# Fetching the filters of a frequency-domain mixer in groups of 16 and 8 rows, with the copies of their halves spread over four engines

## The chip, the cores and the metric

The kernel runs on one core of a Trainium2 chip. The metric is the device time of one execution in microseconds (us), as a median over runs. Five engines work side by side on the core: TensorE (PE: matmuls; PEld is its loading of weights), VectorE (DVE), ScalarE (ACT), GpSimd (POOL) and SyncE (SP), which here only issues transfers. POOL issues transfers too. Each engine takes its instructions strictly in the order in which they were written, and the Tile framework puts semaphore waits between engines.

## The reference

```python
def _attn_ref(x, filt_r, filt_i):              # x: 8 x 3008 x 256; filters: 1505 x 256
    X = np.fft.rfft(x, axis=1)
    Y = X * (filt_r + 1j * filt_i)[None, :, :]
    return np.fft.irfft(Y, n=x.shape[1], axis=1)

def _moe_ref(x, w_gate, w_val, w_out, rms_g):  # 24064 tokens x 256, hidden size 1536
    xn = x / np.sqrt(np.mean(x * x, axis=-1, keepdims=True) + 1e-06) * rms_g
    g = xn @ w_gate
    return (g / (1.0 + np.exp(-g)) * (xn @ w_val)) @ w_out
```

A circular filter along the sequence, done in the frequency domain, is followed by a gated feed-forward network on every token. Inputs and output are float32; the kernel's matmuls take float16.

## The kernel before, in words

The transform of length 3008 = 64 * 47 is split: a matmul with a table of 64 frequencies (`wa`), a transposition, and for each of the 32 values of `k2` a matmul over the 47 others (`wbp`). The result, complex numbers with real parts on partitions 0 to 63 and imaginary parts on 64 to 127, is multiplied by the filter; two products per piece go back through the inverse tables (`wi`), are transposed again, scaled by RMS and sent through the network.

There are 8 sequences. Sequences 1 to 7 are mixed in the gaps of the network's matmuls on the sequence before, by an order written out by hand (`at(slot, ...)`). Sequence 0 has no network to hide behind: everything it needs comes first, and the first matmul of the network (`pg`, L420) follows. All of the change lies in this opening. Its stages:

1. `x_load` (L189, on POOL) fetches sequence 0 with a cast to float16, in eight transfers. SP fetches the tables `tb` and `wbp`.
2. `f_load` (L464 to L473) fetches the filters. For each of four chunks `c` of eight `k2`, and for the real part `fr[c]` and the imaginary part `fi[c]`, one transfer brings 24 rows of 8 KB to every second partition and two transfers bring 12 reversed rows each, in pieces of 1 KB; chunk 0 has one more of 24 rows of 1 KB. `fr` goes through SP, `fi` through POOL, the last `fi` chunk only after the first copies. The other half of each tile is cleared beforehand (L607, L608, L614, L604).
3. `f_dup` (L475 to L480) copies the 64 partitions of `fr[c]` to its upper half and those of `fi[c]` to its lower half: POOL for chunks 0 and 1 and `fi[3]`, ACT for chunk 2 and `fr[3]`.
4. `wi_group` builds the inverse tables; `at_unit` (L486) does the first transform, evicted by ACT (L492) and DVE (L490); `t1_unit` (L509) transposes in eight groups, evicted by DVE (L511) and ACT (L513).
5. `b_unit(0, i)`, i = 0 to 15: two matmuls (L241) into one of four PSUM banks in turn, then the two products with `fr` (L263) and `fi` (L264) of chunk i // 4. They run on DVE, except units 4, 8 and 11, which ACT first copies to SBUF (`v`, L261) and POOL then multiplies.
6. `bit_unit(i)`: sixteen matmuls (L523, L524), two units sharing a pair of PSUM banks; from i = 5 on, every odd i emits the two units five and four steps back; the last four come at the end. ACT evicts them (L532).
7. `t2_unit` (L543), `n_first` (L364), `q_unit` and the scaling lead to the first `pg`. `w_load` (L582, L583, on POOL) fetches the network's weights, the first two thirds after `b_unit(0, 11)`.

`warm_up(n, ...)` issues n matmuls on zeros, 512 columns each, whose results nobody reads.

Of the kernel before, what the change touches and what calls it, by code (L numbers as in the profile page):

```python
# [33 lines left out]
XC = 6  # L34
NXC = H // XC
KC = 8
FC = (8, 8, 8, 8)


def _make_tables():  # L40
    n2 = np.arange(N2)
    wa = np.zeros((P, P))
    wai = np.zeros((P, P))
    for h in range(2):
        for k2 in range(K2):
            c = np.cos(2 * np.pi * ((n2 * k2) % N2) / N2)
            s = np.sin(2 * np.pi * ((n2 * k2) % N2) / N2)
            r = slice(h * 64, h * 64 + 64)
            wa[r, h * 64 + k2] = c
            wai[h * 64 + k2, r] = c * (1.0 if k2 == 0 else 2.0)  # L50
            if k2 == 0:
                alt = 1.0 - 2.0 * (n2 % 2)
                wa[r, h * 64 + 32] = alt
                wai[h * 64 + 32, r] = alt
            else:
                wa[r, h * 64 + 32 + k2] = -s
                wai[h * 64 + 32 + k2, r] = -2.0 * s
    n1 = np.arange(N1)
    wb = np.zeros((KR, K2, P))
    wi = np.zeros((P, 1, 2, P))  # L60
    re, im = slice(0, N1), slice(SL, SL + N1)
    for k2 in range(K2):
        for s in range(48):

            if s < 24:
                k = k2 + 64 * s
                sign, q = 1.0, 16 + 2 * s
            else:
                if k2 and s == 36:
                    continue  # L70
                j = s - 23 if (s < 36 or not k2) else s - 24
                k = 64 * j - (k2 if k2 else 32)
                sign, q = -1.0, 1 + 2 * (s - 24)
            th = 2 * np.pi * ((n1 * k) % N) / N
            c, sn = np.cos(th), np.sin(th)
            if k == 0 or k == NF - 1:
                sn = np.zeros(N1)
            if k2:
                wb[re, k2, q] = c
                wb[im, k2, q] = sign * sn  # L80
                wb[re, k2, HALF + q] = -sn
                wb[im, k2, HALF + q] = sign * c
            else:
                src = re if s < 24 else im
                wb[src, k2, q] = c
                wb[src, k2, HALF + q] = -sn
                m = 1.0 if k in (0, NF - 1) else 2.0
                z = np.zeros(N1)
                g = (m * c, -m * sn)
                gr, gi = (g, (z, z)) if s < 24 else ((z, z), g)  # L90


                for qq, cols in ((re, 0), (im, 1)):
                    wi[q, 0, 0, qq] = (gr, gi)[cols][0]
                    wi[HALF + q, 0, 0, qq] = (gr, gi)[cols][1]
                    wi[q, 0, 1, qq] = (gr, gi)[cols][1]
                    wi[HALF + q, 0, 1, qq] = (gr, gi)[cols][0]
    f = np.float16
    wf = np.zeros((P, K2, P))
    wf[:, 1:, 0:KR] = wb[:, 1:].transpose(2, 1, 0)  # L100
    wf[:, 0] = wi[:, 0, 0]
    wf = (wf * S_INV_B).astype(f)
    ws = np.concatenate([wf[HALF:P], -wf[0:HALF]], 0)
    wai = (wai * S_INV_A).astype(f)
    r = np.arange(KR)
    to_row = (r % 2) * SL + (r // 2 % 2) * H + r // 4
    pm = np.zeros((KR, P))
    pm[r, to_row] = 1.0
    k = np.arange(P)
    ph = (k % 2) * 64 + (k // 2 % 2) * 32 + k // 4  # L110
    tb = np.zeros((P, 7, P), f)
    tb[:, 0] = wa
    tb[:, 1] = np.eye(P)
    tb[0:KR, 2] = pm * S_INV_B
    tb[:, 3] = wf[:, 0]
    tb[:, 4] = ws[:, 0]
    tb[:, 5] = wai[ph]
    tb[:, 6] = wa[:, ph]
    return {"tb": tb, "wb": wb.astype(f), "wbp": wb[to_row].astype(f)}
# [3 lines left out]
def kernel(  # L123
# [39 lines left out]
    pm = tb[0:KR, 2, :]  # L163
    sgn = glob.tile([P, 1], FP32)
    wi = glob.tile([P, 2, K2, P], FP16)
    fr = [glob.tile([P, n, D], FP32, name="fr%d" % c) for c, n in enumerate(FC)]
    fi = [glob.tile([P, n, D], FP32, name="fi%d" % c) for c, n in enumerate(FC)]
    wg = glob.tile([P, 2, DFF], FP16)
    wv = glob.tile([P, 2, DFF], FP16)
    wo = glob.tile([P, JT, D], FP16)  # L170
# [21 lines left out]
    def bank(i, name):  # L192

        pool, tag = ((psM, "mx"), (psG, "pg"), (psV, "pv"), (psB, "mb"), (psO, "po1"), (psO, "po0"))[i]
        return pool.tile([P, 512], FP32, tag=tag, name=name)
# [30 lines left out]
    def wi_at(q, k):  # L226
        return wi[:, q, k, :] if k else tb[:, 3 + q, :]

    def b_unit(b, i):
        if b:  # L230
            ps = bank(3, "psb")
        else:
            ps = bank((0, 3, 4, 5)[i % 4], "psb")
        ps = ps.rearrange("p (a d) -> p a d", a=2)
        for u in range(2):
            k = 2 * i + u
            if b:
                w, t = late_p["wb"], st[b]["t2"][k // KC][:, k % KC, :]
            else:
                w, t = wbp, st[0]["t2"][k // 4][:, k % 4, :]  # L240
            nc.tensor.matmul(ps[:, u, :], w[:, k, :], t, start=True, stop=True)  # L241
        f1, f2 = filt(2 * i, 2)
        if b:
            s1 = late_p["sp"].tile([P, 2, D], FP16, tag="s1", name="s1")
# [9 lines left out]
            ss = xnp.tile([P, 2, 512], FP16, tag="xn", name="ss")  # L254
            s1, s2 = (ss[:, e, :].rearrange("p (a d) -> p a d", a=2) for e in range(2))
        eng = nc.vector
        if (i in (5, 8, 11, 14)) if b else (i in (4, 8, 11)):
            eng = nc.gpsimd
            v = yp.tile([P, 2, 512], FP32, tag="y", name="v")
            v = v[:, 0, :].rearrange("p (a d) -> p a d", a=2)  # L260
            nc.scalar.activation(out=v, in_=ps, func=AXT.Copy)  # L261
            ps = v
# [106 lines left out]
        return y, pss  # L369

    def y_first(y, pss, dh):
        nc.vector.tensor_scalar(out=y[:, dh, :], in0=pss[dh], scalar1=gsb[:, dh:dh + 1],
                                scalar2=None, op0=ALU.mult)

# [81 lines left out]
            nc.sync.dma_start(prev[:, H - 1, :], o3[64:P, 3, :])  # L456


    NC = K2 // KC

    def raw(src, row, ap):
        return bass.AP(tensor=src.tensor, offset=src.offset + row * D, ap=ap)

    def f_load(c, src, t, p0, eng):  # L464
        lo = 1 if c == 0 else 0
        eng.dma_start(t[p0 + 16:p0 + 63:2, :, :].rearrange("p a d -> p (a d)"),
                      raw(src, c * KC, [[64 * D, 24], [1, KC * D]]))
        for g in range(2):
            eng.dma_start(t[p0 + 1 + 24 * g:p0 + 24 + 24 * g:2, lo:KC, :],
                          raw(src, 64 * (1 + 11 * g) - c * KC - lo,  # L470
                              [[64 * D, 12], [-D, KC - lo], [1, D]]))
        if c == 0:
            eng.dma_start(t[p0 + 1:p0 + 48:2, 0, :], raw(src, 32, [[64 * D, 24], [1, D]]))  # L473

    def f_dup(c):  # L475
        for t, a, e in ((fr[c], HALF, 0), (fi[c], 0, HALF)):
            if c == 2 or (c == 3 and a):
                nc.scalar.activation(out=t[a:a + HALF], in_=t[e:e + HALF], func=AXT.Copy)
            else:
                nc.gpsimd.tensor_copy(out=t[a:a + HALF], in_=t[e:e + HALF])  # L480

    def at_unit(m, dh):
        ps = bank(1 + dh, "pat")
# [10 lines left out]
    def t1_unit(g):  # L494
# [4 lines left out]
        else:  # L499
            dst = t3p.tile([KR, 4, D], FP16, tag="t3", name="t2")  # L500
        st[0]["t2"][g] = dst
        pool, tag = ((psO, "po0"), (psO, "po1"), (psM, "mx"), (psB, "mb"))[g % 4]
        ps = pool.tile([P, 4, D], FP16, tag=tag, name="pt1")
        af = aT.rearrange("p a k -> p (a k)")
        for a in range(4):
            for dh in range(2):
                b0 = dh * H * P
                src = af[:, b0:b0 + 32 * P].rearrange("p (i k) -> p k i", k=K2)[:, 4 * g + a, :]
                nc.tensor.transpose(ps[:, a, ts(dh, P)], src, ident)  # L509
        if g % 2 == 0 or g == 7:  # L510
            nc.vector.tensor_copy(out=dst, in_=ps[0:KR])  # L511
        else:
            nc.scalar.activation(out=dst, in_=ps[0:KR], func=AXT.Copy)  # L513
# [72 lines left out]
    with tc.manual_schedule():  # L586
# [26 lines left out]
        for c in range(1, 4):  # L613
            nc.vector.memset(fr[c][0:HALF], 0.0)  # L614
            zero(fi[c][HALF:P])
        for c in range(4):
            f_load(c, filt_r, fr[c], 0, nc.sync)
            if c < 3:
                f_load(c, filt_i, fi[c], HALF, nc.gpsimd)
        with nc.allow_non_contiguous_dma(reason="one gain a partition"):  # L620
            nc.sync.dma_start(gsb, moe_rms_g.rearrange("(a p) -> p a", p=P))

        warm_up(14, 1)
        for g in range(4):
            wi_group(g)
        for m in range(6):
            for dh in range(2):
                at_unit(m, dh)
            for g in ((4, 5), (6,), (7,), (), (), ())[m]:
                wi_group(g)  # L630
        for i in range(8):
            t1_unit(i)
        f_dup(0)
        f_load(3, filt_i, fi[3], HALF, nc.gpsimd)
        f_dup(1)
        for i in range(16):
            if i == 7:
                f_dup(3)
            b_unit(0, i)
            if i % 2 and i >= 5:  # L640
                bit_unit(i - 5)
                bit_unit(i - 4)
            if i == 4:
                f_dup(2)
            if i == 11:
                w_load(0)
                w_load(1)
        for i in range(12, 16):
# [2 lines left out]
        t2_unit(1, 0)  # L651
        warm_up(2, 0)
        first = n_first()
        q_unit(0, 0)
        y_first(*first, 0)
        scale_split(0, 0)
        y_first(*first, 1)
        t2_unit(2, 1)
        t2_unit(3, 0)
        scale_apply(0, 0, 3)  # L660
        t2_unit(4, 0)
# [143 lines left out]
```

## Time and profile before

| What | Value |
|---|---|
| Median of 4 runs | 907.51 us (905.69 to 909.74) |
| The profiled execution, own time | 903.38 us |
| Its span in the trace | 901.6 us, granted clock 0.99 |
| PE busy in the span | 880.2 us (98%) |
| DVE, ACT, POOL busy | 677.1, 619.4, 391.3 us |
| First transposition of `t1_unit` starts | 16.91 us |
| First product of `b_unit(0, 0)` starts on DVE | 22.33 us |
| Last product of `b_unit(0, 15)` ends on DVE | 41.55 us |
| First `pg` matmul of the network starts | 49.71 us |

The profiled execution took 903.38 us, 4.13 us less than the median of the runs; 1.8 us of it lie outside the span. The shares of busy time are averages over the whole span: PE at 98% is the network's work, while the opening of 49.71 us is a different regime that has to be read from the trace itself.

### The profile page before, as it was taken

The numbers are of one execution on the slowest core, as the hardware profiler recorded it, in microseconds if no ns is written. First come the engines' busy times: TensorE is split into PE (matmuls) and PEld (weight loads), VectorE is DVE, ScalarE is ACT, GpSimd is POOL, SyncE is SP. The second block draws the span as 40 slices with busy tenths as digits, with TensorE's granted clock in tenths as the row PEclk, the third lists the DMA queues.
The fourth block names the chain that finished last, engine by engine and source line by source line (L and its number), as shares of the span: only waits on it lengthen the run. The fifth ranks groups of instructions, "written<-read, shape, count | busy, mean of one in ns | idle before, by whom it ended". The sixth has DMA issues, their size and how long they took to land.

```text
span 901.6 us, 17520 instructions
## 1 busy us (share of the span) xinstructions
PE 880.2 (98%) x6329; PEld 561.6 (62%) x6329; DVE 677.1 (75%) x1075; ACT 619.4 (69%) x1047; POOL 391.3 (43%) x353
## 2 busy tenths in 40 slices
PE   8799999999999999999999999999999999999997
PEld 5566666666666666766666666666666666666554
DVE  8766767788988787888688886888878887555554
ACT  8667666677677766887667766787657765676443
POOL 7842730655635552466325552265514551043300
PEclk9699999999999999999999999999999999999999
DMA  9495725674564436444554347332352232331201
GB/s 205 77 185 166 155 57 176 158 172 91 153 178 103 100 79 196 107 95 121 137 139 112 85 98 197 85 96 82 79 168 74 62 89 53 100 68 47 60 24 47
DMA packets 79746, 100.91 MB, mean 112 GB/s; under 512 B 8096, under 2 KB 56416, under 8 KB 79276
## 3 DMA queue, kind: packets, MB, share of 16 engines
q1 hardware_dynamic: 69276, 83.45, 33.6%
q0 software_dynamic: 10384, 16.35, 11.2%
q8 instruction: 49, 0.80, 0.4%
q14 instruction: 37, 0.30, 0.1%
HBM read 67.67 MB, written 46.78 MB: 127 GB/s over the span
## 4 chain that ended last, share of the span: by engine, by line
PE 85%; issue 5%; DMA 4%; ACT 2%; DVE 2%; POOL 2%; SPq 0%; POOLq 0%; ACTq 0%
PE po L437 25%; PE pg L420 25%; PE pv L420 24%; PE psi L286 3%; PE psb L241 3%; PE psn L318 2%; DMA fr<-in_filt_r_dram 2%; PE psa L204 2%; PE psq L339 1%; DVE o L443 1%; DMA g_tmp<-t 1%; DMA rb<-r_tmp 1%; POOL xc L189 0%; ACT sg L424 0%; DVE hh L425 0%
## 5 line engine op out<-in xcount | busy, mean ns | idle before, releaser
L425 DVE TENSOR_TENSOR hh<-pv,sg 128x512 f16<-128x512 f32 (+1 forms) x576 | 391.4, 680 | 202.7 <-ACT sg L424 90.0
L424 ACT ACTIVATE sg<-pg 128x512 f16<-128x512 f32 (+1 forms) x576 | 338.9, 588 | 230.9 <-PE pg L420 222.9
L437 PE MATMUL po<-wo,hh 128*128 128x256 f16 x2256 | 342.2, 272 | 2.3 <-DVE o L443 1.6
L420 PE MATMUL pg<-xn,wg 128*128 128x512 f16 (+1 forms) x1152 | 337.9, 375 | 0.0
L420 PE MATMUL pv<-xn,wv 128*128 128x512 f16 (+1 forms) x1152 | 337.6, 375 | 0.0
L437 PEld LDWEIGHTS <-hh 128*128 128x128 f16 x2256 | 216.5, 98 | 99.2 <-issue 3.6
L277 POOL TENSOR_TENSOR s<-s,s 128x512 f16<-128x512 f16 x96 | 110.5, 1151 | 285.2 <-DVE s L271 202.5
L420 PEld LDWEIGHTS <-wv 128*128 128x128 f16 x1152 | 112.6, 98 | 131.3 <-issue 0.6
L403 POOL TENSOR_TENSOR xn<-y,rb 128x1024 f16<-128x1024 f32 (+1 forms) x45 | 126.0, 2801 | 45.5 <-DMA rb<-r_tmp 33.7
L420 PEld LDWEIGHTS <-wg 128*128 128x128 f16 x1152 | 109.1, 98 | 12.3 <-issue 0.3
L345 POOL TENSOR_TENSOR rho<-u,mhalf 128x4 f32<-128x4 f32 (+1 forms) x48 | 48.9, 1018 | 83.3 <-DVE u L343 83.3
L291 ACT ACTIVATE t<-psi 96x512 f16<-96x512 f32 x112 | 66.4, 593 | 11.5 <-PE psi L286 5.8
L324 ACT ACTIVATE y<-psn,gsb 128x512 f32<-128x512 f32 (+1 forms) x94 | 63.8, 679 | 9.4 <-PE psn L318 2.3
L271 DVE TENSOR_TENSOR s<-psb,fi 64x512 f16<-64x512 f32 x96 | 65.6, 684 | 3.0
L273 DVE SCALAR_TENSOR_TENSOR s<-psb,fi 64x512 f16<-64x512 f32 x96 | 66.5, 693 | 1.3
L247 DVE TENSOR_TENSOR s<-psb,fr 128x512 f16<-128x512 f32 x96 | 65.4, 681 | 0.0
L330 ACT ACTIVATE sq<-psn 128x512 f16<-128x512 f32 (+1 forms) x94 | 54.7, 582 | 0.0
L209 ACT ACTIVATE t<-psa 128x512 f16<-128x512 f32 x70 | 41.8, 597 | 5.6 <-PE psa L204 2.4
L286 PE MATMUL psi<-s,wi 128*128 128x256 f16 x248 | 45.4, 273 | 0.0
L241 PE MATMUL psb<-t,wb 96*128 96x256 f16 x224 | 43.0, 272 | 1.0 <-DVE s L264 0.9
L286 PEld LDWEIGHTS <-wi 128*128 128x128 f16 x248 | 24.2, 98 | 26.5 <-issue 1.4
L318 PEld LDWEIGHTS <-t 128*128 128x128 f16 x368 | 28.3, 98 | 19.8
(97 smaller groups left out, 518.2 us busy)
## 6 DMA issues: line engine op xcount, KB each, us to landing
out_dram<-o SPq DMA_DIRECT2D x84, 256.0 KB
xc<-in_x_dram POOLq DMA_DIRECT2D x56, 192.0 KB, 6.1
z_tmp<-t SPq DMA_DIRECT2D x28, 384.0 KB
t<-z_tmp SPq DMA_DIRECT2D x28, 384.0 KB
g_tmp<-t SPq DMA_DIRECT2D x56, 192.0 KB
rb<-r_tmp SPq DMA_DIRECT2D x41, 256.0 KB
t<-g_tmp SPq DMA_DIRECT2D x21, 384.0 KB
out_dram<-o SPq DMA_DIRECT2D x12, 192.0 KB
```

Source lines behind the costliest of these rows:

```text
L241: nc.tensor.matmul(ps[:, u, :], w[:, k, :], t, start=True, stop=True)
L247: nc.vector.tensor_tensor(out=s1, in0=ps, in1=f1, op=ALU.mult)
L271: nc.vector.tensor_tensor(out=s2[a], in0=ps[e], in1=f2[e], op=ALU.mult)
L273: nc.vector.scalar_tensor_tensor(out=s2[a], in0=ps[e], scalar=-1.0, in1=f2[e], op0=ALU.mult, op1=ALU.mult)
L277: nc.gpsimd.tensor_tensor(out=s, in0=s1, in1=s2, op=ALU.add)
L286: nc.tensor.matmul(ps[:, u, :], wi_at(q, 2 * i + u), ss[q][:, u, :], start=(q == 0), stop=(q == n - 1))
L291: nc.scalar.activation(out=st[b]["t3"][c][:, 2 * r:2 * r + 2, :], in_=ps[0:KR], func=AXT.Copy)
L403: nc.gpsimd.tensor_tensor(out=xv, in0=yv, in1=rv.unsqueeze(1).to_broadcast([P, 2, n, P]), op=ALU.mult)
L420: nc.tensor.matmul(ps[:, 0:w], wt[:, dt_, ts(jt, P)], xn[:, dt_, 0:w], start=(dt_ == 0), stop=(dt_ == 1))
L424: nc.scalar.activation(out=sg[:, 0:w], in_=pg[:, 0:w], func=AXT.Silu)
L425: nc.vector.tensor_tensor(out=hh[:, 0:w], in0=pv[:, 0:w], in1=sg[:, 0:w], op=ALU.mult)
L437: nc.tensor.matmul(po[s4 // 2][:, s4 % 2, :], hh[:, ts(s4, P)], wo[:, jt, :], start=(jt == 0 and s4 % 2 == 0), stop=(jt == JT - 1 and (s4 ...
```

## The change

`f_load` now fetches both parts of a chunk together, in a group of 16 rows through SP (one transfer of 16 rows of 8 KB and one of 16 reversed rows for each part) and a group of 8 rows through POOL (the same two for each part). One reversed row is still fetched twice; it is now the sixteenth in place of the twelfth, so the table row that carries nothing moves from s = 36 to s = 40. All four chunks are issued ahead of the computation, and the gains `gsb` ahead of them. The copies are called one by one, on ACT, POOL or, for `fr[3]`, as a transfer on SP. Six matmuls of `warm_up` stand before `at_unit(4, 0)`. The first four `b_unit`s' matmuls (`b_mm`) stand between the transposition groups 1 and 2, and groups 4 to 7 come after the products of units 0 and 1. Units 3, 7, 10 and 13 go to POOL in place of 4, 8 and 11. The weights' first two thirds are fetched after unit 13. In the tail `y_first` for the second half and `t2_unit(2)` go from DVE to ACT.

```diff
-        if (i in (5, 8, 11, 14)) if b else (i in (4, 8, 11)):
+        if (i in (5, 8, 11, 14)) if b else (i in (3, 7, 10, 13)):
...
     def y_first(y, pss, dh):
+        if dh:
+            nc.scalar.activation(out=y[:, dh, :], in_=pss[dh], func=AXT.Identity, scale=gsb[:, dh:dh + 1])
+            return
...
-    def f_load(c, src, t, p0, eng):
...
+    def f_load(c):
         lo = 1 if c == 0 else 0
+        for g, n, eng in ((0, 16, nc.sync), (16, 8, nc.gpsimd)):
+            for src, t, p0 in ((filt_r, fr[c], 0), (filt_i, fi[c], HALF)):
+                q = p0 + 16 + 2 * g
+                eng.dma_start(t[q:q + 2 * n - 1:2, :, :].rearrange("p a d -> p (a d)"),
+                              raw(src, c * KC + 64 * g, [[64 * D, n], [1, KC * D]]))
+                q = p0 + 1 + 2 * g
+                eng.dma_start(t[q:q + 2 * n - 1:2, lo:KC, :],
+                              raw(src, 64 * max(g, 1) - c * KC - lo, [[64 * D, n], [-D, KC - lo], [1, D]]))
+                if c == 0 and g:
+                    eng.dma_start(t[p0 + 1:p0 + 48:2, 0, :], raw(src, 32, [[64 * D, 24], [1, D]]))
...
+    def f_dup(c, e, eng):
+        t = (fr, fi)[e][c]
+        a, o = (0, HALF) if e else (HALF, 0)
+        if eng is nc.scalar:
+            eng.activation(out=t[a:a + HALF], in_=t[o:o + HALF], func=AXT.Copy)
+        elif eng is nc.sync:
+            eng.dma_start(t[a:a + HALF], t[o:o + HALF])
+        else:
+            eng.tensor_copy(out=t[a:a + HALF], in_=t[o:o + HALF])
...   (t1_unit)
-        pool, tag = ((psO, "po0"), (psO, "po1"), (psM, "mx"), (psB, "mb"))[g % 4]
+        pool, tag = ((psG, "pg"), (psV, "pv"))[g % 2]
...
-        if g % 2 == 0 or g == 7:
+        if g not in (1, 4):
             nc.vector.tensor_copy(out=dst, in_=ps[0:KR])
...
+        for c in range(4):
+            f_load(c)
...
         for m in range(6):
+            if m == 4:
+                warm_up(6, 0)
...
+        A, G, S = nc.scalar, nc.gpsimd, nc.sync
+        t1_unit(0)
+        t1_unit(1)
+        ps0 = [b_mm(0, i) for i in range(4)]
+        t1_unit(2)
+        t1_unit(3)
+        f_dup(0, 0, A)
+        f_dup(0, 1, G)
+        f_dup(1, 1, G)
+        f_dup(3, 0, S)
         for i in range(16):
+            if i == 5:
+                f_dup(2, 0, A)
+                f_dup(2, 1, G)
+            b_unit(0, i, ps0[i] if i < 4 else None)
+            if i == 0:
+                t1_unit(4)
+                t1_unit(5)
+            elif i == 1:
+                t1_unit(6)
+                t1_unit(7)
+            elif i == 3:
+                f_dup(1, 0, A)
+            elif i == 10:
+                f_dup(3, 1, A)
             if i % 2 and i >= 5:
                 bit_unit(i - 5)
                 bit_unit(i - 4)
-            if i == 11:
+            if i == 13:
                 w_load(0)
                 w_load(1)
...
         first = n_first()
+        y_first(*first, 1)
         q_unit(0, 0)
         y_first(*first, 0)
         scale_split(0, 0)
-        y_first(*first, 1)
-        t2_unit(2, 1)
+        t2_unit(2, 0)
```

More of the change, by code (lines that the diff above doesn't have):

```diff
@@ L36 @@
 KC = 8
-FC = (8, 8, 8, 8)
 def _make_tables():
@@ L68, in _make_tables @@
             else:
-                if k2 and s == 36:
+                if k2 and s == 40:
                     continue
-                j = s - 23 if (s < 36 or not k2) else s - 24
+                j = s - 23 if (s < 40 or not k2) else s - 24
                 k = 64 * j - (k2 if k2 else 32)
@@ L165 @@
     wi = glob.tile([P, 2, K2, P], FP16)
-    fr = [glob.tile([P, n, D], FP32, name="fr%d" % c) for c, n in enumerate(FC)]
-    fi = [glob.tile([P, n, D], FP32, name="fi%d" % c) for c, n in enumerate(FC)]
+    fr = [glob.tile([P, KC, D], FP32, name="fr%d" % c) for c in range(K2 // KC)]
+    fi = [glob.tile([P, KC, D], FP32, name="fi%d" % c) for c in range(K2 // KC)]
     wg = glob.tile([P, 2, DFF], FP16)
@@ L227, in wi_at, with b_mm @@
         return wi[:, q, k, :] if k else tb[:, 3 + q, :]
[L229 to L234, printed above, removed]
+    def b_mm(b, i):
+        ps = bank(3 if b else (0, 3, 4, 5)[i % 4], "psb").rearrange("p (a d) -> p a d", a=2)
         for u in range(2):
@@ L241, in b_unit @@
             nc.tensor.matmul(ps[:, u, :], w[:, k, :], t, start=True, stop=True)
+        return ps
+    def b_unit(b, i, ps=None):
+        if ps is None:
+            ps = b_mm(b, i)
         f1, f2 = filt(2 * i, 2)
@@ L456, in o_store @@
             nc.sync.dma_start(prev[:, H - 1, :], o3[64:P, 3, :])
-    NC = K2 // KC
     def raw(src, row, ap):
         return bass.AP(tensor=src.tensor, offset=src.offset + row * D, ap=ap)
-    def f_load(c, src, t, p0, eng):
+    def f_load(c):
         lo = 1 if c == 0 else 0
[L466 to L480, printed above, removed]
+        for g, n, eng in ((0, 16, nc.sync), (16, 8, nc.gpsimd)):
[17 more added lines that the diff above has]
+            eng.tensor_copy(out=t[a:a + HALF], in_=t[o:o + HALF])
     def at_unit(m, dh):
@@ L615 @@
             zero(fi[c][HALF:P])
[L616 to L619, printed above, removed]
         with nc.allow_non_contiguous_dma(reason="one gain a partition"):
             nc.sync.dma_start(gsb, moe_rms_g.rearrange("(a p) -> p a", p=P))
+        for c in range(4):
+            f_load(c)
         warm_up(14, 1)
@@ L630 @@
                 wi_group(g)
[L631 to L635, printed above, removed]
-        for i in range(16):
-            if i == 7:
-                f_dup(3)
-            b_unit(0, i)
+        A, G, S = nc.scalar, nc.gpsimd, nc.sync
[8 more added lines that the diff above has]
+        f_dup(3, 0, S)
+        for i in range(16):
+            if i == 5:
[12 more added lines that the diff above has]
+                f_dup(3, 1, A)
             if i % 2 and i >= 5:
@@ L642 @@
                 bit_unit(i - 4)
-            if i == 4:
-                f_dup(2)
-            if i == 11:
+            if i == 13:
                 w_load(0)
```

## The prediction

> **What bounds the kernel now.** I read the timeline of PE first. Its first network matmul stands here:
>
> ```profile
> 16.91 0.28 PE L509 MATMUL pt<-tb,aT 128*128 128x128 f16 x1 [0.51 <-ACT aT L492]
> ...
> 49.71 1.10 PE L420 MATMUL pg<-xn,wg 128*128 128x512 f16 x2
> ```
>
> From there on the chain of waits is one PE piece after the other, and no edit touches work behind it that PE waits for. So the change is worth what it moves 49.71 us, and nothing else. The same view shows the last back-mixing matmul (L524) ending at 42.3; 7.4 us of tail follow. The stretch before it has no steady bound. By the table of busy time in stretches:
>
> ```profile
> 16.00:20.00 4.00, 3.34 (x50) 3.04 (x48) 2.65 (x4) 2.29 (x4) 2.32 (x4) 1.00 0.90 211
> 20.00:24.00 4.00, 2.87 (x34) 2.24 (x33) 3.45 (x6) 1.62 (x2) 3.94 (x4) 1.00 0.78 190
> 24.00:28.00 4.00, 2.27 (x26) 1.42 (x25) 4.00 (x7) 1.96 (x2) 3.90 (x4) 0.88 0.92 184
> 28.00:40.00 12.00, 10.00 (x91) 7.82 (x90) 9.00 (x16) 9.37 (x15) 10.32 (x9) 0.50 0.05 10
> ```
>
> (Stretch, length, busy PE, PEld, DVE, ACT, POOL, PE's granted clock, DMA share, GB/s.) DMA is full until 28 us, then silent; DVE is nearly full from 22 to 40, POOL fuller. DVE's timeline has 26 products, one each 0.60 us, so 15.6 us of work between 22.33 and 41.55: 19.2 us, of which 3.1 are idle, 1.61 of them for POOL's unit 8. POOL's own order is the key to the change:
>
> ```profile
> 12.74 0.63 POOL L469 DMA_DIRECT2D fi<-in_filt_i_dram  x1
> 14.70 0.59 POOL L469 DMA_DIRECT2D fi<-in_filt_i_dram  x1 [1.33 <-DMA xc<-in_x_dram]
> 15.88 0.54 POOL L466 DMA_DIRECT2D fi<-in_filt_i_dram  x1 [0.59 <-ACT aT L492]
> 16.91 0.58 POOL L469 DMA_DIRECT2D fi<-in_filt_i_dram  x1 [0.49 <-DMA fi<-in_filt_i_dram]
> 17.80 0.57 POOL L469 DMA_DIRECT2D fi<-in_filt_i_dram  x1 [0.30 <-DMA fi<-in_filt_i_dram]
> 19.25 1.91 POOL L480 COPY fr<-fr 64x2048 f32<-64x2048 f32 x1 [0.89 <-DMA fr<-in_filt_r_dram]
> 21.22 1.89 POOL L480 COPY fi<-fi 64x2048 f32<-64x2048 f32 x1
> ```
>
> See the waits in front of issues. Counted through, the 15th transfer of POOL waits for its 7th (an `xc`, issued at 4.9, 10.0 us to landing), the 16th for the 8th (so "ACT aT" is a misnamed releaser), the 17th for the 9th, the 18th for the 10th. So each queue holds eight transfers: number n is not issued before n - 8 has landed, and everything behind it in POOL's order waits too.
>
> **What the skill says.** The Trainium skill, "DMA: Bandwidth & Descriptors", section "Why a DMA increments its semaphore by 16 and not by 1": a transfer uses the largest number of the 16 engines, up to 16, that divides its slowest dimension. Then 24 and 12 rows use 12, 16 rows all, 8 rows half. The trace lists no single engine; shares of 0.78 to 0.92 with both queues loaded agree with it but don't prove it. Same page, "Issuing engines are not separate DMA queues": all queues share the engines, so moving a transfer saves only issue time; agreed, the two queues moved 0.81 and 0.91 MB in 12 to 20 us. "TensorE: Matmul & The Clock Gate", "Part 1: The HAM clock gate": PE falls to half rate when idle; agreed, clock 0.50 from 28 to 40, matmuls of 96 columns 0.08 us apart in place of 0.04.
>
> **The change part by part.** Call T the time when the `fi[0]` copy is done; now 23.1, just as DVE asks (second product at 23.14).
>
> *Transfers.* Same bytes plus 0.5 MB for the copy by SP. Over 16 engines instead of 12 the end at 28.5 may come up to 2 us earlier; chunk 3's imaginary part no longer waits for POOL's copies (issue at 23.05). SP issues 16 transfers at 0.79 us from 7.76 with its own waits for eight back: `fi[0]`'s last at some 11 us, landing near 20 by the 8 to 9 us that `fr[0]` takes now. Nothing behind SP is urgent: its copy of `fr[3]`, after a landing by 30, ends by 34, and unit 12 comes after 36. `gsb` ahead: in 24 to 28, with `gsb`, SP's queue took 60.5% for 0.44 MB against 49.7% for the same in 16 to 20; 0.108 of 4 us is 0.4 us, now in front of `x`.
>
> *POOL's queue, where I look for the loss.* It issues 18 filter transfers in place of 10 ahead of its first copy. From 9.88: six to 13.3 us. The 15th and 16th wait for `x` as now, 14.7 and 15.85, plus 0.3 for `gsb`. Ten more at 0.57 us end at 22.3 if nothing else waits: the lower bound. But the last four wait for the 15th to 18th, issued at 15 to 17.4; with the shortest landing now shown, 6.4 us, and the 0.57 us of the last issue that is 24.4; with a queue half as deep as now, where a chunk's group is 64 KB instead of 192 or 96, perhaps 23. I take 23.5. The `fi[0]` copy adds 1.9: T = 25.5 (24.2 to 26.3), 2.4 us later than now. Behind it on POOL stand the copy of `fi[1]`, unit 3, the copy of `fi[2]`; on DVE everything behind unit 0's second product.
>
> *PE's front.* Six warm-up matmuls, 0.22 each at full clock (PE `psa`, also 512 columns), are 1.3 us; 0.56 of that lies in the present wait for `x`. First transposition near 17.5, not 16.9. Groups 0 to 3 with `b_mm` between (waiting 1.02 us for ACT's eviction of group 1), DVE reaches unit 0 at 22.3: as now. Hidden behind T.
>
> *DVE after T.* Second product of unit 0, 0.6; evictions of groups 5, 6, 7, 1.8; 11 units of 1.2, 13.2: 15.6 us. PE at half clock needs 2.2 us for each two units (4 products at 0.21, 16 small at 0.08), so unit 14's matmuls, behind the back-mixing of 8 and 9, come 0.9 late. DVE ends at T + 16.5. The freed unit (12 on DVE for 13) and the vanished idle are in that.
>
> *POOL after T.* Copies 2 x 1.9, unit 3 at 2.5: T + 6.4; units 7 and 10 to T + 12.6. Unit 13's `v` stands on ACT behind the new copy of `fi[3]` (1.9) and two evictions, ready T + 13.9; done T + 16.4. Last back-mixing: unit 13, then 14 and 15, T + 17.2 (full clock) to T + 18.3 (half). I take T + 17.8 = 43.3, against 42.3: **+1.0 us**.
>
> *ACT's copies.* `fr[0]`, `fr[1]`, `fr[2]` wait for landings by 18, 22.5, 26: all before DVE needs them (22, T + 4.8, T + 8.4). Nothing.
>
> *Tail.* `y_first` and `t2_unit(2)` leave DVE; but DVE's `xn` at 48.88 starts as `psr` ends (48.85), so 0 gained, 0.1 at most. `w_load` starts near T + 16.4 = 41.9, not 39.57; six issues of 0.78 end at 46.6, `rho` needs POOL near 47.4: covered, by 0.8 us only. The first `wg` lands 4.2 us after issue (shortest shown), 46.1; covered. A cooler PE in the tail could add 0.3. I book +0.1.
>
> Sum: +1.1 us. The profiled execution would go from 903.38 to 904.5; its offset to the median (4.1 us) stays, so 907.51 becomes **908.6 us**.
>
> **Rivals.**
> 1. *Slower: landings rule.* With the queues filled early, transfers 15 to 18 take the longest landing now shown, 8.6 us, rather than 6.4. POOL's last issue ends at 26.6, T = 28.5, back-mixing at 46.3: +4.0, with half a clock at the end up to +5; 911.5 to 912.5. For it: `fi` landings of 7.8 to 8.6 us at just this time now. Against: POOL's groups are a third to two thirds of the size. It decides from T = 27.3 on (27.3 + 17.8 - 42.3 = 2.8).
> 2. *Faster: POOL at its bare issue.* Shorter lists at 0.5 us and no landing waited for: last issue at 21.6, T = 23.5, and DVE bounds: 23.5 + 16.5 and the last unit's matmuls 0.7 make 40.7, -1.6; 905.9. With PE fast as well, -2.8.
> 3. *Faster: T doesn't bind.* If `x` lands early enough for POOL to be free by 20.5, DVE runs from 22.3 without a gap: 22.9 + 15.6 + 0.7 = 39.2, -3.1; with the tail 904.3. Against: 18 issues of 0.5 us from 9.88 alone reach 18.9, and `x` lands at 14.7.
> 4. *Doesn't do what it says*: the 8-row transfers on 8 engines each leave DMA no faster. This touches only the transfers' 2 us, already off the path.
>
> **How the numbers follow.** A measurement of this kernel tells some 0.3% (2.7 us) from no change. Main case 0.55, own range 906 to 911; rival 1 0.22; rival 2 0.13; rival 3 0.10. Slower by more: 0.19 of rival 1 and 0.05 of the main case, 0.24. Faster by more: 0.07 of rival 3, 0.04 of 2, 0.02 of the main case (PE and DMA better than booked), 0.13. Same: 0.63. The range runs from rival 3's 904.3 to rival 1's upper 912.5, leaving some 0.1 out on either side.
>
> **What would show it.** Right: in POOL's timeline, 18 filter issues with waits, last ending at 23 to 24.5; the first filter copy on POOL after that; DVE idle 2 to 3 us ahead of the second product of unit 0; then DVE gapless but for unit 14; `pg` at 50.3 to 51.3. Wrong: that copy before 22 us, DVE idle for a filter's landing (DMA `fr` or `fi` as releaser) at units 4, 8 or 12, or the clock under 0.7 as the network starts.

## The result, and the profile after

The changed kernel takes 909.21 us in the median of 36 runs (906.19 to 913.13), the kernel before 905.75 us in 55 runs beside it (903.53 to 909.74). The ratio is **1.0039, 95% interval 1.0031 to 1.0047**. At the 907 us of the prediction that is +3.5 us (2.8 to 4.3): slower, by a little more than the 0.3% named as the bound. The profiled executions took 903.38 us before and 908.16 us after; their first `pg` matmul starts at 49.71 and at 53.37 us, 3.7 us apart, so most of the 4.8 us between these two executions lies in the opening (for the rest see the last section). The stretch from the last back-mixing matmul to `pg` is 7.0 us (7.4 before).

The timeline of PE in the changed kernel (start, duration, instruction, idle time before it and its releaser):

```profile
9.20 0.50 PE L568 MATMUL pst<-tb,wbp 96*128 96x128 f16 x3 [2.70 <-DMA wbp<-wbp_t]
...
23.20 0.28 PE L515 MATMUL pt<-tb,aT 128*128 128x128 f16 x1 [0.51 <-ACT aT L498]
...
53.37 0.38 PE L423 MATMUL pg<-xn,wg 128*128 128x512 f16 x1 [0.22 <-DVE xn L395]
```

Two things look late at once: the first transposition by 6.3 us, with a wait of 2.70 us for a table ahead of it, and `pg` by 3.7 us. It is tempting to make the first the cause of the second. The timeline of POOL has a second candidate:

```profile
15.87 0.50 POOL L470 DMA_DIRECT2D fr<-in_filt_r_dram  x1 [1.19 <-DVE wi L573]
16.95 0.63 POOL L473 DMA_DIRECT2D fr<-in_filt_r_dram  x1 [0.58 <-DMA xc<-in_x_dram]
18.00 0.51 POOL L470 DMA_DIRECT2D fi<-in_filt_i_dram  x1 [0.41 <-ACT aT L498]
18.88 0.61 POOL L473 DMA_DIRECT2D fi<-in_filt_i_dram  x1 [0.38 <-DMA fr<-in_filt_r_dram]
...
23.78 0.51 POOL L470 DMA_DIRECT2D fr<-in_filt_r_dram  x1 [1.08 <-DVE aT L496]
24.65 0.61 POOL L473 DMA_DIRECT2D fr<-in_filt_r_dram  x1 [0.37 <-DMA fr<-in_filt_r_dram]
25.62 0.51 POOL L470 DMA_DIRECT2D fi<-in_filt_i_dram  x1 [0.36 <-issue]
26.16 0.61 POOL L473 DMA_DIRECT2D fi<-in_filt_i_dram  x1
26.81 3.79 POOL L486 COPY fi<-fi 64x2048 f32<-64x2048 f32 x2
```

Count POOL's transfers: the first four lines are the 15th to 18th, the next four the 23rd to 26th, its last filter transfers. Each of these starts 7.9, 7.7, 7.6 and 7.3 us after the one eight places ahead of it. The copies of `fi[0]` and `fi[1]` stand behind them and begin at 26.81, so T, the time when the `fi[0]` copy is done, is about 28.7 us (26.81 and half of the pair's 3.79), against 23.1 before.

By the table of busy time in stretches (stretch, length, busy PE, PEld, DVE, ACT, POOL, PE's granted clock, DMA share, GB/s):

```profile
16.00:20.00 4.00, 4.00 (x50) 3.27 (x51) 2.56 (x4) 2.52 (x6) 2.14 (x5) 0.60 1.07 198
20.00:24.00 4.00, 3.34 (x37) 2.33 (x36) 2.60 (x5) 2.26 (x4) 2.44 (x5) 1.00 1.04 212
24.00:28.00 4.00, 3.49 (x35) 2.97 (x34) 0.98 (x2) 2.94 (x2) 3.20 (x5) 0.75 0.71 178
28.00:40.00 12.00, 8.48 (x119) 7.22 (x117) 11.84 (x21) 9.23 (x13) 9.95 (x8) 0.94 0.24 51
```

DVE was full in 24 to 28 before (4.00 of 4); now it has 0.98 there and is full only afterwards, 11.84 of 12. DVE's products were moved back as a block. In this execution the block's start can't be assigned to either candidate. DVE's timeline:

```profile
29.16 0.68 DVE L263 TENSOR_TENSOR ss<-psb,fr 128x512 f16<-128x512 f32 x1
29.76 0.68 DVE L264 TENSOR_TENSOR ss<-psb,fi 128x512 f16<-128x512 f32 x1
```

Its first product starts at 29.16, because the transpositions were late, and its second at 29.76, about 1 us after the copy of `fi[0]` was made. Which of the two costs the time is what the experiments settle.

### The profile page after: what moved, and what is told of

Its sections match the earlier page's. It is cut to its first block, busy times and chain, and to the rows that moved or that the text cites. A ratio compares the mean times of both kernels' runs of the same rounds, so it can differ in the third digit from the quotient of the medians.

```text
span 906.4 us, 17556 instructions
## 1 busy us (share of the span) xinstructions
PE 880.3 (97%) x6335; PEld 561.8 (62%) x6335; DVE 675.7 (75%) x1072; ACT 621.8 (69%) x1050; POOL 393.0 (43%) x358
## 4 chain that ended last, share of the span: by engine, by line
PE 87%; issue 5%; DMA 3%; DVE 3%; ACT 1%; POOL 1%; SPq 0%; DVEq 0%; POOLq 0%; ACTq 0%
PE po L440 25%; PE pg L423 25%; PE pv L423 24%; PE psb L236 3%; PE psi L286 3%; PE psn L318 2%; PE psa L203 2%; DMA g_tmp<-t 1%; DMA wbp<-wbp_t 1%; PE psq L339 1%; DVE o L446 1%; PE pt L515 1%; DMA rb<-r_tmp 1%; PE pst L565 0%; ACT sg L427 0%
```

## The experiments

Every ratio below is against the kernel before, run beside it on the same chip; the figure in us is at 907 us. The runs were made in four rounds on three chips, so runs of different rounds are compared only through the kernel before. Times of single steps come from one profiled execution each.

### Table or queue: runs a, b, c, d

Theory Q: POOL's filter issues, each held by the landing of the transfer eight ahead of it, keep the `fi[0]` copy back. Theory G: the transfer of the gains, now the first of its kind on SP, delays the table and with it PE. Run a takes the changed kernel and fetches the gains after the filters:

```diff
-        with nc.allow_non_contiguous_dma(reason="one gain a partition"):
-            nc.sync.dma_start(gsb, ...)
         for c in range(4):
             f_load(c)
+        with nc.allow_non_contiguous_dma(reason="one gain a partition"):
+            nc.sync.dma_start(gsb, ...)
```

> The changed kernel with the gains gsb fetched after the filters, as before the change. Theory G (the 256 four-byte pieces of gsb, queued right behind the table wbp, hold up wbp from about 6.9 to 9.15 us, PE sits idle, falls to half clock and starts its transpositions at 23.2 instead of 17.5): wbp lands near 6.9 us, transpositions start near 17.5, DVE's second product of unit 0 waits for POOL's copy of fi[0] at about 27, first pg at 50.5 to 51.5, time 1.5 to 3 us under the changed kernel, still 0.5 to 2 us over the kernel before. Rival Q (only POOL's queue of 18 transfers makes the loss, gsb costs 0.4 us as the prediction booked): time 0.4 us under the changed kernel, about 3 us over before. Rival N (the changed order of products is good and gsb alone spoils it): 3 us or more faster than before.

Measured: 1.0043 (1.0026 to 1.006), +3.9 us: as slow as the full change. PE's, POOL's and DVE's timelines of run a:

```profile
17.48 0.28 PE L515 MATMUL pt<-tb,aT 128*128 128x128 f16 x1 [0.51 <-ACT aT L498]
```
```profile
26.56 3.72 POOL L486 COPY fi<-fi 64x2048 f32<-64x2048 f32 x2
```
```profile
22.55 0.68 DVE L263 TENSOR_TENSOR ss<-psb,fr 128x512 f16<-128x512 f32 x1
28.48 0.69 DVE L264 TENSOR_TENSOR ss<-psb,fi 128x512 f16<-128x512 f32 x1 [5.25 <-POOL fi L486]
```

Here PE's front is on time, DVE makes its first product at 22.55, almost as before the change (22.33), and then stands for 5.25 us, with the copy of `fi` on POOL as the releaser. The late front isn't needed for the loss. The same trace tells what held the copy. The last part of `fi[0]` was issued on POOL at 13.13 and took 8.0 us to landing, so its data was complete at 21.1, but the copy began at 26.56. POOL's eight last issues lie in between, from 17.45 to 26.51: some 4.5 us of issuing (0.51 or 0.61 us each) and 4.6 us of waiting. An estimate from these figures: with the issuing alone the copy could have begun near 22, so most of the delay is the waits for landings and not the number of issues. Run b is the reverse, the kernel before with the gains fetched ahead of the filters:

```diff
+        with nc.allow_non_contiguous_dma(reason="one gain a partition"):
+            nc.sync.dma_start(gsb, ...)
         for c in range(4):
             f_load(c, filt_r, fr[c], 0, nc.sync)
...
-        with nc.allow_non_contiguous_dma(reason="one gain a partition"):
-            nc.sync.dma_start(gsb, ...)
```

> The kernel before with one edit: gsb fetched ahead of the filters, as in the changed kernel. Theory G: wbp lands about 2.3 us later, PE at half clock while it builds the inverse tables, transpositions start at 22 to 23 instead of 16.9, the products follow without their present idle time, pg 3 to 5 us later, time 3 to 5 us over the kernel before. Rival Q: 0.4 us over.

Measured: 1.0002 (0.9987 to 1.0017). G falls on both sides. Runs c and d move one instruction: POOL copies `fi[0]` between the issues of chunk 1 and those of chunk 2, ahead of eight transfers. Run d is the changed kernel with that alone, run c is run a with it:

```diff
         for c in range(4):
+            if c == 2:
+                f_dup(0, 1, nc.gpsimd)
             f_load(c)
...
-        f_dup(0, 1, G)
```

> The changed kernel with gsb after the filters and POOL's copy of fi[0] issued between the transfers of chunks 1 and 2 instead of behind all four. If POOL's queue is the second limit: the copy ends near 21, DVE's products run from 22.5 us almost without a gap, pg near 47.5 to 48.5, time 1 to 2.5 us under the kernel before. If POOL's queue does not bind once gsb is last: equal to the run with gsb last alone, within 0.5 us.

> The changed kernel with only POOL's copy of fi[0] issued between the transfers of chunks 1 and 2; gsb stays first. Theory G: PE is late anyway and DVE reaches unit 0 at 29.2 us only because of it, so nothing moves: 0 to 0.7 us under the changed kernel. Rival Q (POOL's queue is the whole loss): 3 us under the changed kernel, equal to before.

Measured: c 1.0003 (0.9992 to 1.0014), d 1.0001 (0.9987 to 1.0015). Moving one copy takes the 3.5 us back. Run c met neither of its two forecasts: it was not faster than the kernel before, and not as slow as run a. The timelines of POOL and of DVE in run d:

```profile
21.15 1.95 POOL L486 COPY fi<-fi 64x2048 f32<-64x2048 f32 x1 [3.01 <-issue]
```
```profile
23.30 0.68 DVE L264 TENSOR_TENSOR ss<-psb,fi 128x512 f16<-128x512 f32 x1
...
29.36 0.69 DVE L264 TENSOR_TENSOR ss<-psb,fi 128x512 f16<-128x512 f32 x1 [0.61 <-POOL fi L486]
```

The copy now stands 3.01 us until the last part of `fi[0]` has landed and is done at 23.1, at the same time as before the change; DVE's wait of 5.25 us is gone, and 0.61 us come back at unit 4, for the copy of `fi[1]`, which still stands behind all eight. **Q holds**: the loss against the kernel before is the place of the `fi[0]` copy behind POOL's held issues. It is not the whole price of the new fetch, as run h below shows: there the changed order with the old fetch is faster by another 2.7 us. In run d DVE's block, from the first product to the last, takes 18.7 us with 2.1 us of gaps; in run h it takes 16.2 us with none.

### The two halves of the change: runs g and h

Run g is the kernel before with the new fetch alone: the new `f_load` (and its table row), all four chunks issued ahead, every copy, unit and transposition as before.

```diff
-            f_load(c, filt_r, fr[c], 0, nc.sync)
-            if c < 3:
-                f_load(c, filt_i, fi[c], HALF, nc.gpsimd)
+            f_load(c)
...
-        f_load(3, filt_i, fi[3], HALF, nc.gpsimd)
```

> The kernel before with the new fetch alone: groups of 16 rows on SP and 8 rows on POOL, all four chunks ahead of the computation (with the table row they need); copies, order of products and POOL's units as before. Theory Q (each transfer on POOL ahead of its first copy waits for the landing of the one eight before it): POOL's last filter transfer ends near 26.5 us, its copies of fr[0] and fi[0] at 28.5 and 30.5, DVE starts at 28.5 instead of 22.3, loses its present idle time of 3 us, first pg 3 to 6 us later, time 3 to 6 us over before. Rival (the fetch over all engines lands sooner and pays): equal or faster.

Run h is the changed kernel with the old fetch (the old `f_load` and its table row, not shown), everything else as changed:

```diff
-            f_load(c)
+            f_load(c, filt_r, fr[c], 0, nc.sync)
+            if c < 3:
+                f_load(c, filt_i, fi[c], HALF, nc.gpsimd)
...
         f_dup(0, 1, G)
+        f_load(3, filt_i, fi[3], HALF, nc.gpsimd)
         f_dup(1, 1, G)
...
```

> The changed kernel with the fetch of the kernel before (fr through SP, fi through POOL, 24 and 12 rows, the last fi chunk after POOL's copy of fi[0]), keeping the spread copies, the products between the transpositions and four units on POOL. Theory Q: the order itself is sound; the copy of fi[0] ends near 21.5, DVE runs from 22.5 with little idle, first pg at 47 to 49, time 1 to 3 us under before. Rival (PE at half clock and units 10 and 13 on POOL eat it): within 1 us of before.

Measured: g **1.0047** (1.0032 to 1.0061), +4.3 us; h **0.9971** (0.9959 to 0.9983), -2.6 us. DVE's timeline in run g, then POOL's in run h:

```profile
28.89 0.69 DVE L263 TENSOR_TENSOR ss<-psb,fr 128x512 f16<-128x512 f32 x1 [4.24 <-POOL fr L482]
...
30.84 0.69 DVE L264 TENSOR_TENSOR ss<-psb,fi 128x512 f16<-128x512 f32 x1 [1.25 <-POOL fi L482]
```
```profile
21.61 1.88 POOL L484 COPY fi<-fi 64x2048 f32<-64x2048 f32 x1 [0.21 <-DMA fi<-in_filt_i_dram]
...
25.13 1.91 POOL L484 COPY fi<-fi 64x2048 f32<-64x2048 f32 x1
```

In run g both copies of chunk 0 stand behind POOL's last issue, which ends at 26.95, and DVE waits for each of them. In run h POOL has ten filter issues ahead of its first copy, as before the change, and is free at 21.6 us. (In this execution `x` was late: the first transposition starts at 19.56 and `pg` at 51.08, outside the forecast of 47 to 49. Run k below, with the same order, has `pg` at 47.26.) So the change is a loss and a gain in one: the fetch costs about 4 us, the order around it wins 2.6. The two add to +1.7 us with an error of about the same size; measured together they are +3.5 (2.8 to 4.3), so whether they simply add is not settled.

### Repairs of the fetch: runs i and j

Run i is run d with the last chunk's 8-row groups on SP, so that POOL issues four fewer; run j is run d without the six warm-up matmuls.

```diff
-        for g, n, eng in ((0, 16, nc.sync), (16, 8, nc.gpsimd)):
+        for g, n, eng in ((0, 16, nc.sync), (16, 8, nc.sync if c == 3 else nc.gpsimd)):
```

> The changed kernel with POOL's copy of fi[0] between chunks 1 and 2 (run d), and chunk 3's groups of 8 rows on SP instead of POOL. Theory Q: POOL's copy of fi[1] moves from 27.4 to 25.2, DVE's wait of 0.6 at unit 4 goes, unit 7 and 13 come earlier, time 0.5 to 1.5 us under run d and under before. Rival (SP's own queue of eight holds chunk 3 back, so the copy of fr[3] by transfer is late for unit 12): 0 to 2 us over run d.

```diff
-            if m == 4:
-                warm_up(6, 0)
```

> Run d without the six warm-up matmuls ahead of at_unit(4, 0). If they only fill the wait for x: transpositions start 0.3 to 0.8 us earlier, nothing else moves since DVE waits for POOL's copy, 0 to 0.5 us under run d. Rival (they keep PE's clock up through the transpositions): matmuls of the transpositions 1.5 to 2 times as long, 1 us or more over run d.

Measured: i 0.9983 (0.9967 to 0.9998), -1.5 us; j 1.0002 (0.9986 to 1.0019). In run i the `fi[1]` copy starts at 26.42 in place of 27.43 (25.2 was forecast). That fewer issues on POOL help further is not shown: the interval lies under 1, but overlaps that of run d. The warm-up changes nothing that can be measured.

### What in the order wins the 2.6 us: runs k, l, m, n

All four start from run h. Run k fetches the gains last; run l puts units 4, 8 and 11 on POOL again, with the weights' fetch after unit 11; run m makes all transpositions ahead of the products; run n puts the copies back where they were.

Run l:

```diff
-        if (i in (5, 8, 11, 14)) if b else (i in (3, 7, 10, 13)):
+        if (i in (5, 8, 11, 14)) if b else (i in (4, 8, 11)):
...
-            if i == 13:
+            if i == 11:
```

Run m (groups 4 to 7 also leave their places after units 0 and 1):

```diff
-        t1_unit(0)
-        t1_unit(1)
-        ps0 = [b_mm(0, i) for i in range(4)]
-        t1_unit(2)
-        t1_unit(3)
+        for i in range(8):
+            t1_unit(i)
...
```

Run n:

```diff
-        f_dup(0, 0, A)
+        f_dup(0, 0, G)
         f_dup(0, 1, G)
         f_load(3, filt_i, fi[3], HALF, nc.gpsimd)
+        f_dup(1, 0, G)
         f_dup(1, 1, G)
-        f_dup(3, 0, S)
...
-                f_dup(2, 1, G)
+                f_dup(2, 1, A)
+            if i == 7:
+                f_dup(3, 0, A)
+                f_dup(3, 1, G)
...
-                f_dup(1, 0, A)
...
-                f_dup(3, 1, A)
```

> Run h (the changed order with the fetch of before) with gsb after the filters. If the gains ahead cost the 0.4 us of engine time that the prediction booked, or nothing: within 1 us of run h. If they delay x and the tables (in h's profile PE waited 1.9 us more for x): 1 to 2 us under run h, 3 to 5 us under before.

> Run h with units 4, 8 and 11 on POOL, as before, in place of 3, 7, 10 and 13, and the weights fetched after unit 11. DVE gets one unit more, 1.2 us; POOL ends earlier. If DVE bounds the products: 0.5 to 1.5 us over run h. If unit 13 on POOL is what ends last (in h DVE ends at 42.4, POOL at 42.3): within 0.5 us of run h.

> Run h with all eight transposition groups ahead of the products, as before; the spread copies stay. If putting products between the transpositions is what gains: 1 to 2.5 us over run h, equal to before. If it gains nothing (DVE does the same evictions and products either way, from the same start): within 0.7 us of run h.

> Run h with the copies where the kernel before has them: fr[0], fi[0], fr[1], fi[1] and fi[3] on POOL, fr[2], fi[2] and fr[3] on ACT, none by transfer. If the spread copies are what gains (POOL ends the copy of fi[0] 2 us sooner and reaches its first unit 4 us sooner): 1.5 to 3 us over run h, equal to before. If not: within 0.7 us of run h.

| Run | Ratio, 95% interval | At 907 us |
|---|---|---|
| h, order alone | 0.9971 (0.9959 to 0.9983) | -2.6 |
| k, h with the gains last | 0.9970 (0.9958 to 0.9983) | -2.7 |
| l, h with three units | 0.9967 (0.9954 to 0.9979) | -3.0 |
| m, h with transpositions first | 0.9980 (0.9970 to 0.9990) | -1.8 |
| n, h with copies as before | 0.9997 (0.9987 to 1.0007) | -0.3 |

The place of the gains and the fourth unit on POOL make no difference that can be told from the noise. The order of the transpositions may be worth 0.8 us; the intervals of h and m overlap, so this stays open. With the copies back in their places the gain is gone: **spreading the copies over the engines is what wins**, about 2.4 us (1.0 to 3.8, an estimate from the two intervals). (They stand on three engines, ACT, POOL and SP, not on four as the title has it.) Run n moves five copies at once, so which of them wins it is not shown. POOL's and DVE's timelines of run n show where the time goes:

```profile
20.67 1.89 POOL L484 COPY fr<-fr 64x2048 f32<-64x2048 f32 x1 [0.40 <-DMA fr<-in_filt_r_dram]
22.61 1.93 POOL L484 COPY fi<-fi 64x2048 f32<-64x2048 f32 x1
...
30.14 1.26 POOL L263 TENSOR_TENSOR sg<-v,fr 128x512 f16<-128x512 f32 x1
```
```profile
33.96 0.69 DVE L263 TENSOR_TENSOR ss<-psb,fr 128x512 f16<-128x512 f32 x1 [0.79 <-issue]
...
39.56 0.69 DVE L263 TENSOR_TENSOR ss<-psb,fr 128x512 f16<-128x512 f32 x1 [1.74 <-PE psb L236]
```

POOL makes the copy of `fr[0]` ahead of that of `fi[0]` again, its first unit starts at 30.14 (28.18 in run h), and DVE has gaps of 0.79, 1.74 and, at 41.62, 0.77 us. Ahead of the gap of 1.74 us PE waited 0.96 us, at 38.30, for the `hh` of a unit on POOL, and the matmuls that DVE needed came behind that. In run h DVE has no gap over 0.3 us from 26.27 to 42.49. Run h's products began late, when more had landed; but run k's, in the same order, begin at 23.06, a little earlier than run n's at 24.01, and run up to 39.28 without a gap too.

Runs h, k and l are faster than the kernel before by 0.3% each, and so also than the changed kernel, though they were not run beside it. Their intervals lie on each other, so none of the three is the best.

## Why the prediction was right or wrong

**The path was right.** The prediction looked for the loss in POOL's queue: POOL's issues held by landings, the `fi[0]` copy behind them, DVE's second product behind that. Runs a and d show just this. The steps from T on hold in the profile after: DVE's last product ends at 45.38, T + 16.7 (predicted 16.5); POOL's unit 13 ends at 45.19, T + 16.5 (16.4); the last back-mixing matmul ends at 46.40, T + 17.7 (17.8). The end was set by POOL: PE waits 1.01 us, at 45.25, for the `hh` of unit 13. DVE's agreement is partly luck. The prediction had 15.6 us of work and 0.9 us of waiting for a PE at half clock; in the profile after PE ran at 0.94 in 28 to 40, DVE worked without a gap, and it began 1.0 us after T because the front was late. In run a, where it began at once, it ended at T + 15.7. The tail became 0.4 us shorter, where 0.1 us longer was booked.

**One term was mis-sized: the end of POOL's last issue**, 23.5 us in the prediction (22.3 to 24.4), 26.8 in the profile after, 26.5 in run a and 26.95 in run g. That makes T 28.7 in place of 25.5, and rival 1, the rule of landings, which had 26.6, 28.5 and 46.3, meets every step within 0.2 us. Its time, +4 to +5 us, lies at the upper end of the measured +3.5 (2.8 to 4.3); the main case's +1.1 lies well below. So the likeliest case of the prediction was not the one that came, and most of the chance was put on "no change" where the kernel got slower by 0.39%.

The step that failed is the sentence "with a queue half as deep as now ... perhaps 23". It let POOL's landings shrink with POOL's own groups. The issues of DMA in 12 to 20 us, after the change (tile, queue, count, KB each, median us from issue to landing), under the line of what moved:

```profile
DMA packets 1125, 1.74 MB, mean 218 GB/s; under 512 B 343, under 2 KB 874, under 8 KB 1036
...
fi<-in_filt_i_dram POOLq DMA_DIRECT2D x3, 64.0 KB, 7.1
fr<-in_filt_r_dram POOLq DMA_DIRECT2D x3, 64.0 KB, 7.4
```

and the same view of the kernel before:

```profile
DMA packets 892, 1.74 MB, mean 217 GB/s; under 512 B 273, under 2 KB 629, under 8 KB 789
...
fi<-in_filt_i_dram POOLq DMA_DIRECT2D x2, 192.0 KB, 8.0
fi<-in_filt_i_dram POOLq DMA_DIRECT2D x4, 96.0 KB, 8.2
```

The bytes in these 8 us are the same, 1.74 MB. Transfers of a third to two thirds of the size land only about a tenth sooner. In run a, with the same fetch and again 218 GB/s in 12 to 20 us, they land no sooner at all:

```profile
fr<-in_filt_r_dram POOLq DMA_DIRECT2D x4, 64.0 KB, 7.8
fi<-in_filt_i_dram POOLq DMA_DIRECT2D x3, 64.0 KB, 8.5
```

An estimate from the lines of the two kernels: both queues share one rate, so a landing takes what is outstanding on both, divided by that rate. After, eight transfers of 128 KB on SP and eight of 64 KB on POOL are some 1.6 MB, and at 218 GB/s 7.2 us; the lines have 7.1 to 7.4. With the same eight on POOL at an average of 128 KB, as before, it would be 9.6 us, where 8.0 to 8.2 are shown, and run a's 7.8 to 8.5 lie above its 7.2, so the sum is rough. But it offers a reason why halving POOL's groups did not halve its landings: what SP had outstanding stayed. When SP had issued its last filter transfer, at 21.7, POOL's landings did get short (these are of 24 to 28 us), and too late:

```profile
fr<-in_filt_r_dram POOLq DMA_DIRECT2D x2, 64.0 KB, 5.0
fi<-in_filt_i_dram POOLq DMA_DIRECT2D x2, 64.0 KB, 3.8
```

That SP's emptying queue is the reason is argued from the times; no run isolates it. In the profile after, a part of the 3.3 us comes from the start of the chain: the 18th transfer was issued at 18.88, where 17.4 was taken, since `x` landed later in this execution, and the 26th 7.3 us after it, where an end at 23.5 would need 5.5. Run a tells the two apart: there the 18th was issued at 16.84, before the time taken, the 17th and 18th took 8.5 and 8.6 us to land, and the last issue ended at 26.5 all the same. So it is the landings that were mis-sized, and the 8.6 us of rival 1 is what run a shows; in the profile after rival 1 met the end through a later start and shorter landings, which is luck.

**The sixteen engines.** The prediction took from the Trainium skill ("DMA: Bandwidth & Descriptors", "Why a DMA increments its semaphore by 16 and not by 1") that 16 rows use all engines and 24 rows use 12, and booked up to 2 us for it at the end of the fetch. The passage also names an exception on this chip for some transfers that GpSimd issues, which the prediction left out, so 8 engines for POOL's 8 rows are not certain by the page either. The rate in 12 to 20 us didn't move, 217 and 218 GB/s. The last filter transfer of the profile after, issued at 26.16, took 3.6 us and landed at 29.8; before, issued at 24.17, it took 6.4 us and landed at 30.6 (the prediction's 28.5 is where the DMA share falls off); in run g, with the new fetch, it landed at 31.3. So no gain of 2 us is seen, and the 0.8 us of the one pair is within the scatter of single executions. Whether more engines took part the trace doesn't list. Rival 4 expected DMA to be no faster; that came, but whether for its reason is not shown.

**Edits booked at little.** The gains ahead, 0.4 us: within noise (runs a and b). The warm-up, 1.3 us, of which 0.56 hidden: within noise (run j). The copies on ACT, nothing: right, and the prediction missed their other side, that POOL and the units behind it gain. They were priced only inside the case where T is late, and there they are covered. Rival 3, T not binding, gave -3.1 us; run h, which takes the held issues away and leaves the rest, measured -2.6, run l -3.0. So the size of what the order wins was in the prediction, in the case that the fetch rules out, and by that case's path: DVE without a gap from 23.06 to 39.28 in run k.

**The late front** was not foreseen: in the profile after, PE waits 2.70 us for the table and the first transposition starts at 23.20, not 17.5. Run a has 17.48 and is as slow, so it isn't needed for the loss.

**The clock.** The prediction took the 0.50 in 28 to 40 us as agreeing with a PE that falls to half rate when idle. Its table doesn't show an idle PE: it was busy 10.00 of these 12 us, and 2.27 of the 4 us before them. In run k the same stretch has a clock of 1.00 with PE busy 8.44 of 12 us. What sets the clock there stays open.

## What to carry to other kernels

On an engine that both issues transfers and computes, count every issue ahead of its first computing instruction: with eight in flight, as in these traces, issue n waits for the landing of n - 8, and the copy behind it waits too. Cutting transfers into smaller ones lengthens that line, and can leave the landings nearly as they were (7.1 to 8.5 us for 64 KB here, against 8.0 to 8.2 for 96 and 192 KB before). When a copy is urgent, put it ahead of the transfers that aren't (one moved line took 3.5 us back), or give it to an engine that issues none; and where a change holds two ideas, run each alone before dropping both, since here one was worth -2.6 us.

## What was not expected of the hardware

- The landing of a transfer on POOL's queue depended little on its size while both queues were loaded: medians of 7.1 to 7.7 us for 24 to 64 KB after, 7.2 to 8.2 us for 24 to 192 KB before, all issued in 12 to 20 us. It differed as much between executions: 7.5 to 8.5 us for 24 to 64 KB in run a, and 8.2 to 9.8 us for 24 to 192 KB in run h.
- The same opening starts at quite different times in single executions: over the fourteen kernels' profiles the first transposition starts between 16.91 and 23.20 us, and PE's waits for `x` or for the table ahead of it reach 3.19 us (run j, which is no slower than the kernel before). The profile of the kernel before happens to be the earliest of all fourteen, so a single pair of profiles overstates any delay ahead of the transpositions.
- The prediction expected that the change is worth what it moves the first `pg`, "and nothing else". In single executions that doesn't hold. In the profile after, PE waits once more in the network on sequence 0:

```profile
119.03 0.38 PE L236 MATMUL psb<-t,wb 96*128 96x256 f16 x2 [1.67 <-ACT v L261]
```

ACT itself had waited 2.30 us there for a transfer (`g_tmp`); 0.70 us before the change, where PE doesn't wait. No edit touches this place, and the wait isn't tied to the change: 0.39 us in run b and 1.24 in run g, none in run j, 1.92 in run k, whose execution took 904.85 us though its `pg` starts 2.4 us earlier than that of the kernel before. What makes it long or short stays open.
- PE's granted clock in 28 to 40 us was 0.50 in the profile before and 0.94 in the profile after, which is the slower kernel.
